# Loading batch 1's k and v after w1's last quarter, and splitting one transpose step of batch 0's q in two

## The chip, the cores and the metric

The kernel runs on one core of a Trainium2 chip. The metric is the device time of one execution in microseconds (us); lower is better. Before the change three runs took 293.19, 293.66 and 294.61 us, a median of 293.66 us. One further execution was recorded by the hardware profiler; all durations below are from it.

## What is computed

The reference is an attention without a score matrix, followed by a two-layer block with a residual. Inputs are q, k, v of shape (8 batches, 8 heads, 576 rows, 64), a gain of 512 and two weight matrices, all in float32.

```
q_s = softmax(q, over the 64 columns)         k_s = softmax(k, over the 576 rows)
kv  = einsum('bhsd,bhse->bhde', k_s, v)       x = einsum('bhsd,bhde->bhse', q_s, kv), heads side by side: (8, 576, 512)
xn  = (x - mean) / sqrt(var + 1e-6) * g_ln    out = x + max(xn @ w_ch1, 0) @ w_ch2     (512 -> 2048 -> 512)
```

## The kernel before the change

**Tiling.** A batch's first 512 rows are four tiles of 128 rows (`j` = 0 to 3). Its last 64 rows, the left-over, are joined with those of the next batch to a fifth tile. Per batch the steps are: softmax of k (maximum over the rows, with a reduction over partitions on GpSimd, subtraction, exponential), `pkv` (the matrix kv of each head on TensorE), softmax of q, transposes of q so that `po` can multiply it by kv, then `x`, `xn`, the transposes `xT`, the first layer `l1`, its `relu`, the second layer `l2`, the final scaling `put` and the `store`. Matmuls run in bfloat16.

**Weights.** `w1l.0` to `w1l.3` load w1 in four quarters of 512 columns, and `w2l.0` to `w2l.3` load w2 in four quarters of 512 rows, each 1 MB of float32 in DRAM, cast to 512 KB of bfloat16 on the way. They are issued by GpSimd (POOL), on a queue of their own (software queue q0). k, v, q and the outputs travel on the queues of SyncE (SP, q1) and ScalarE (ACT, q10). For batch 0 the first layer uses w1 as loaded and the gain is put on the transposed x; afterwards `w1s.0` to `w1s.3` multiply w1's quarters by the gain in place, for all later batches.

**Order.** The order of all work is written out by hand: the string `PROGRAM` is a list of words such as `l2.0.4` or `kl.1.0@SP` (step, batch or chunk, index, and the engine where there is a choice). The words are issued in this order, each to its engine's own instruction stream, and each engine works its stream strictly in order. So a word that has to wait holds back whatever comes after it on the same engine, and nothing on others unless they need its result.

Words that matter here, with the line that the profile shows for them:

- `kl.1.0` (L145) and `vl.1.0` (L151): 1 MB each, batch 1's k and v; `kll.1`, `vll.1` (L124): their left-over rows, 128 KB each; `ql.1.0` (L168): 1 MB of batch 1's q.
- `kmax.1.0` (L184, L187), `kmaxl.1.0` (L194): maximum of batch 1's k on VectorE (DVE); `kar.1.0` (L199): the reduction over partitions on POOL; `ksub.1.1`, `ksub.1.0`, `ksub.1.2` (L217): the subtractions on DVE; `kexp.1.*` (L241): exponentials on ACT; `vc.1.*` (L109): v to bfloat16; `pkv.1.*` (L394).
- `qT.1.2` (L372): transposes of q on TensorE (PE); `qTe.1.2` (L109): their copy out of PSUM on DVE; `zpe.1.2` (L361): eight small matmuls that read this copy and give the softmax sums.
- `l1.0.*` (L552), `l2.0.*` (L592): first and second layer of batch 0. `l2.0.0` to `l2.0.3` read w2's first quarter, `l2.0.4` to `l2.0.7` its second, and so on.
- `w1l` (L511), `w2l` (L530), `w1s` (L519).
- `qT.0.1` (L332), `qTe.0.1` (L109), `zpe.0.1` (L345), `kvb.0.1` (L404, L407): q of batch 0, column chunks 2 and 3, and the normalised kv.
- `warm` (L621): matmuls without a use for their result, which keep PE running.
- `gate.i` (L523): a DMA of 32 bytes on SP that reads a value which another step writes. SP waits for that step before it issues the DMA, and so does all that stands behind it in SP's stream. `gate.2` reads w1's last quarter, so it waits for `w1l.3`.

On PE the words of interest follow each other as `l1.0.14.0, l2.0.0, qT.1.2, l2.0.1, l2.0.2, l2.0.3, zpe.1.2, l2.0.4, ..., l2.0.7, pkv.1.0, pkv.1.1, l2.0.8, ...`; on POOL as `w1l.3, w2l.0, w2l.1, kar.1.0, w2l.2, w2l.3, vc.1.1`.

Of the kernel before, what the change touches and what calls it, by code (L numbers as in the profile page):

```python
# [20 lines left out]
def kernel(  # L21
# [606 lines left out]
    PE, DV, AC, PO, SP = "PE", "DV", "AC", "PO", "SP"  # L628
# [12 lines left out]
        po.0.3 g.1 x.0.0 po.0.1 po.0.2 g.2@AC x.0.3 xn.0.0@AC x.0.1 xn.0.3@AC warm.11.128 xT.0.0  # L641
        xU.0.0 xTe.0.0@DV xTf.0.0@AC warm.4.128 xT.0.3 xU.0.3 xn.0.1@DV l1.0.0.0 xTe.0.3@DV
        xTf.0.3@AC xT.0.1 xU.0.1 x.0.2 l1.0.0.3 xTf.0.1@AC xTe.0.1@DV relu.0.0.0 xn.0.2@DV
        l1.0.0.1 kll.1@AC qmax.1.0 relu.0.0.3 qsub.1.0 xT.0.2 xU.0.2 relu.0.0.1 l1.0.1.1 xTe.0.2@AC xTf.0.2@DV l1.0.1.0 qmax.1.2
        relu.0.1.1 l1.0.1.3 qexp.1.0 qsub.1.2 l1.0.1.2 relu.0.1.3 relu.0.1.0 l1.0.0.2 sq.0.1
# [6 lines left out]
        pkv.1.0 pkv.1.1 kl.2.0@AC l2.0.8 kvb.1.0 l2.0.9 kl.3.0@AC po.1.1 po.1.3 sq.0.0 po.1.2  # L652
        x.1.1 po.1.0 l2.0.10 rstd.0 x.1.0 xn.1.1@AC l2.0.11 x.1.2 xn.1.0@AC x.1.3 l2.0.12
        vl.2.0@AC xn.1.2@AC l2.0.13 qmax.2.0 xT.1.0 put.0.0 l2.0.14 xTe.1.0@AC xn.1.3@DV put.0.1
        l2.0.15 put.0.2 l1.1.0.0 put.0.3 xT.1.2 kmax.2.0 store.0.3@SP l1.1.1.0 xTe.1.2@AC vll.2@SP
        l1.1.2.0 ql.3.0@SP relu.1.0.0 qsub.2.0 l1.1.3.0 relu.1.2.0 relu.1.1.0 l1.1.8.0 kmaxl.2.0
        relu.1.3.0 qmax.2.2 l1.1.9.0 kar.2.0 relu.1.8.0 qexp.2.0 l1.1.10.0 qsub.2.2 relu.1.9.0
        l1.1.11.0 qTd.2.0 ksub.2.2 l1.1.12.0 ksub.2.0 relu.1.11.0 qTd.2.1 relu.1.10.0 l1.1.13.0
        qexp.2.2 ksub.2.1 l1.1.14.0 relu.1.12.0 qTd.2.2 zq.2.0 l1.1.15.0 relu.1.13.0 relu.1.14.0
        l1.1.0.2 qTd.2.3 relu.1.15.0 zq.2.2 l1.1.1.2 relu.1.0.2 kexp.2.1 qll.1.1@SP l1.1.2.2  # L660
        vc.2.1 store.0.0@SP kexp.2.2 l1.1.3.2 store.0.2@SP vc.2.0 kexp.2.0 store.0.1@SP qmax.3.0
        l2.1.0 vc.2.2 qll.1.0@SP relu.1.2.2 l2.1.1 kmax.3.0 relu.1.1.2 kll.3@SP relu.1.3.2 pkv.2.0
        kll.4@SP sq.1.2 pkv.2.1 vl.3.0@SP l2.1.2 kvb.2.0 vll.3@AC l2.1.3 qmax.3.2 po.2.0 po.2.2
        po.2.3 l2.1.4 x.2.0 x.2.3 l2.1.5 xn.2.0@AC x.2.2 xn.2.3@AC xT.2.0 po.2.1 l2.1.6 sq.1.1
        x.2.1 vc.3.2 l2.1.7 qmax.1.4 xn.2.2@AC xT.2.3 kmaxl.3.0 sq.1.3 l2.1.8 xn.2.1@DV sq.1.0
        kar.3.0 xT.2.2 qsub.3.0 l2.1.9 sq.2.0 l2.1.10 xT.2.1 qsub.1.4 rstd.1 qexp.3.0 ksub.3.1
        l2.1.11 kl.4.0@SP sq.2.2 l2.1.12 put.1.0 qTd.3.0 kexp.3.1 l2.1.13 put.1.1 vc.3.1 put.1.2
        qexp.1.4 l2.1.14 vc.3.0 qTd.1.4 l2.1.15 l1.2.0 qTd.3.1 put.1.3 l1.2.1 ksub.3.2 relu.2.0
        ql.4.0@SP ksub.3.0 store.1.1@AC l1.2.2 relu.2.1 l1.2.3 kexp.3.2 qsub.3.2 relu.2.2 l1.2.4
        relu.2.3 kexp.3.0 l1.2.5 kmax.4.0 l1.2.6 relu.2.4 qexp.3.2 l1.2.7 relu.2.5 zq.1.4 qTd.3.3  # L670
        pkv.3.0 relu.2.6 pkv.3.1 store.1.3@AC po.1.4 kvb.3.0 l1.2.8 qTd.3.2 relu.2.7 l1.2.9
        kmaxl.4.0 relu.2.8 ql.5.0@SP zq.3.0 l1.2.10 kar.4.0 gate.3 relu.2.9 store.1.0@SP l1.2.11
        x.1.4 po.3.1 l1.2.12 relu.2.11 zq.3.2 vll.6@SP relu.2.10 vl.4.0@SP l1.2.13 relu.2.12 x.3.1
        sq.2.3 l1.2.14 ksub.4.1 relu.2.13 po.3.2 vll.4@SP po.3.3 xn.1.4@AC l1.2.15 x.3.3
        store.1.2@AC po.3.0 x.3.2 relu.2.14 l2.2.0 gate.0 relu.2.15 ksub.4.0 l2.2.1 sq.3.2
        qmax.4.0 xn.3.1@AC l2.2.2 xn.3.3@AC xT.3.1 l2.2.3 x.3.0 sq.2.1 xn.3.0@DV l2.2.4 qsub.4.0
        rstd.2 xT.3.3 xn.3.2@AC l2.2.5 sq.3.0 ksub.4.2 xT.3.0 l2.2.6 kexp.4.2 l2.2.7 qexp.4.0
        l2.2.8 kexp.4.1 xT.3.2 put.2.1 l2.2.9 qmax.4.2 sq.3.3 kl.5.0@SP vc.4.1 l2.2.10 sq.1.4
        qsub.4.2 kll.5@SP sq.3.1 l2.2.11 vc.4.0 store.2.1@SP l2.2.12 put.2.2 l2.2.13 put.2.0
        store.2.2@SP vc.4.2 l2.2.14 qmax.5.0 qTd.4.0 l2.2.15 l1.3.0 put.2.3 l1.3.1 zq.4.0 relu.3.0  # L680
        qexp.4.2 l1.3.2 qsub.5.0 kexp.4.0 l1.3.3 qTd.4.2 l1.3.4 qmax.5.2 relu.3.1 qTd.4.3 relu.3.2
        pkv.4.0 relu.3.4 zq.4.2 pkv.4.1 relu.3.3 l1.3.5 qTd.4.1 l1.3.6 kvb.4.0 kl.6.0@SP l1.3.7
        kmax.5.0 relu.3.6 kll.6@SP relu.3.5 vl.5.0@SP l1.3.8 relu.3.7 po.4.0 store.2.0@AC l1.3.9
        kmaxl.5.0 relu.3.8 x.4.0 l1.3.10 kar.5.0 relu.3.9 rstd.3 po.4.1 po.4.3 qexp.5.0 l1.3.11
        x.4.1 x.4.3 relu.3.10 l1.3.12 ksub.5.0 relu.3.11 l1.3.13 relu.3.12 sq.4.0 po.4.2 l1.3.14
        x.4.2 xn.4.1@AC l1.3.15 kmax.6.0 relu.3.14 xT.4.1 relu.3.13 l2.3.0 relu.3.15 gate.1 l2.3.1
        xn.4.0@AC kmaxl.6.0 qTd.5.1 qll.3.0@AC l2.3.2 ksub.5.2 xn.4.2@AC xn.4.3@DV qTd.5.0 l2.3.3
        ksub.5.1 sq.4.3 l2.3.4 qsub.5.2 kexp.5.1 xT.4.2 kar.6.0 l2.3.5 qll.3.1@AC put.3.0 vll.5@SP
        l2.3.6 kexp.5.0 store.2.3@SP vc.5.0 ksub.6.2 l2.3.7 xT.4.3 kexp.5.2 kll.7@AC l2.3.8
        put.3.1 qexp.5.2 xT.4.0 l2.3.9 zq.5.0 l2.3.10 qTd.5.3 qmax.3.4 l2.3.11 vc.5.2 vl.6.0@SP  # L690
        l2.3.12 vc.5.1 ql.6.0@SP put.3.2 l2.3.13 qsub.3.4 ksub.6.1 l2.3.14 l2.3.15 kexp.6.1 l1.4.0
        put.3.3 pkv.5.0 relu.4.0 pkv.5.1 sq.4.2 l1.4.1 kvb.5.0 l1.4.2 relu.4.1 zq.5.2 l1.4.3
        vc.6.0 relu.4.2 qexp.3.4 po.5.0 ksub.6.0 po.5.3 vc.6.1 relu.4.3 l1.4.4 qTd.3.4 po.5.1
        zq.3.4 l1.4.5 relu.4.4 qTd.5.2 x.5.0 l1.4.6 vc.6.2 relu.4.5 x.5.3 kexp.6.0 kl.7.0@SP
        l1.4.7 x.5.1 qll.5.1@SP l1.4.8 kexp.6.2 qmax.6.0 ql.7.0@SP relu.4.6 l1.4.9 relu.4.8
        relu.4.7 pkv.6.0 xn.5.1@AC pkv.6.1 po.3.4 relu.4.9 l1.4.10 xT.5.1 x.3.4 l1.4.11 kvb.6.0
        relu.4.10 xT.1.4 l1.4.12 qmax.6.2 relu.4.11 sq.4.1 l1.4.13 store.3.0@SP kmax.7.0 relu.4.12
        qll.5.0@SP po.5.2 l1.4.14 relu.4.13 gate.2 rstd.4 store.3.1@SP l1.4.15 store.3.2@AC x.5.2
        l2.4.0 xn.5.0@DV relu.4.15 kmaxl.7.0 relu.4.14 l2.4.1 qsub.6.2 xn.5.2@AC kar.7.0 l2.4.2
        l2.4.3 ksub.7.1 l2.4.4 store.3.3@AC xn.5.3@AC qsub.6.0 xT.5.0 l2.4.5 kexp.7.1 l2.4.6  # L700
        qmax.7.0 xT.5.3 sq.5.0 l2.4.7 qexp.6.2 xT.5.2 l2.4.8 put.4.1 l2.4.9 put.4.0 qTd.6.2
        qmax.7.2 store.4.0@AC l2.4.10 sq.5.2 l2.4.11 qll.7.0@AC qexp.6.0 l2.4.12 put.4.2 l2.4.13
        qTd.6.0 l2.4.14 qTd.6.1 l2.4.15 l1.5.0 put.4.3 qTd.6.3 l1.5.1 ksub.7.2 relu.5.0 qsub.7.0
        vll.7@SP vl.7.0@AC l1.5.2 store.4.1@SP relu.5.1 l1.5.3 store.4.2@AC qmax.5.4 relu.5.2
        ksub.7.0 l1.5.4 sq.5.3 l1.5.5 relu.5.3 zq.6.0 relu.5.4 l1.5.6 zq.6.2 l1.5.7 relu.5.6
# [477 lines left out]
```

## Time and profile before

| | |
|---|---|
| median of three runs | 293.66 us |
| the profiled execution: its time, its span | 293.68 us, 291.9 us |
| PE busy | 283.0 us (97% of the span) |
| DVE, ACT, POOL busy | 183.3, 172.4, 47.7 us |
| read from and written to DRAM | 36.70 MB, 9.44 MB |
| granted TensorE clock, mean | 1.000 |

The span runs from the first to the last instruction; 1.8 us of the time lie outside it. Times in the views are counted from the span's start. Busy shares are averages over the whole execution: what the change is worth is read from the first 45 us, in which the transfers of batch 0, of batch 1 and of the weights go on together.

### The profile page before, as it was taken

To read this page: it belongs to the slowest core of one execution; us is meant where nothing else is said; L and a number is where in the kernel's file an instruction comes from. 1 tells how busy PE (TensorE), PEld (TensorE's weight loads), DVE (VectorE), ACT (ScalarE), POOL (GpSimd) and SP (SyncE) were. 2 spreads that over 40 slices of the span, in tenths; PEclk is the share of its full clock that TensorE was granted. 3 is DMA by queue.
4 is the path that set the end of the run, shared out by engine and by line. 5 is a ranking of instruction groups with operands and counts; after the bars stand their busy time and mean duration, and the time that the engine had idled before them with its cause. 6 is when DMAs were issued, how large, how long until landed. Compare 5 with 4: busy or idle time off the path is not lost.

```text
span 291.9 us, 4998 instructions
## 1 busy us (share of the span) xinstructions
PE 283.0 (97%) x1952; PEld 145.5 (50%) x1952; DVE 183.3 (63%) x309; ACT 172.4 (59%) x322; POOL 47.7 (16%) x48
## 2 busy tenths in 40 slices
...
GB/s 214 335 247 233 239 222 299 351 224 207 213 225 212 300 197 251 157 274 169 236 166 285 234 121 234 25 98 109 120 19 50 78 124 40 66 42 36 2 30 115
DMA packets 78144, 49.62 MB, mean 170 GB/s; under 512 B 44580, under 2 KB 73640, under 8 KB 78120
## 3 DMA queue, kind: packets, MB, share of 16 engines
...
q10 hardware_dynamic: 12888, 10.36, 12.0%
...
HBM read 36.70 MB, written 9.44 MB: 158 GB/s over the span
## 4 chain that ended last, share of the span: by engine, by line
PE 84%; DMA 12%; POOL 1%; SPq 1%; issue 0%; DVE 0%
PE pc L592 40%; PE ph L538 33%; DMA w_sb<-in_moe_w_ch_dram 9%; PE ph L552 5%; DMA vt<-in_v_dram 3%; PE pot L419 2%; PE pk L394 2%; PE pc L570 1%; POOL v_ab L109 0%; PE pot L428 0%; SPq L174 0%; SPq L145 0%; PE pxt L474 0%; POOL w_sb L530 0%; POOL w_sb L511 0%
## 5 line engine op out<-in xcount | busy, mean ns | idle before, releaser
L592 PE MATMUL pc<-w_sb,hT 128*128 128x512 bf16 x560 | 123.8, 379 | 0.2 <-DMA w_sb<-in_moe_w_ch_dram 0.2
L544 ACT ACTIVATE hT<-ph 128x512 bf16<-128x512 f32 x112 | 63.6, 595 | 60.5 <-PE ph L538 59.9
L538 PE MATMUL ph<-xnT_ab,w_sb 128*128 128x512 bf16 x384 | 87.2, 379 | 0.0
L592 PEld LDWEIGHTS <-hT 128*128 128x128 bf16 x560 | 54.2, 98 | 63.8 <-DMA w_sb<-in_moe_w_ch_dram 0.4
L538 PEld LDWEIGHTS <-w_sb 128*128 128x128 bf16 x448 | 42.8, 98 | 48.7 <-issue 0.2
L602 DVE SCALAR_TENSOR_TENSOR ot<-pc,rstd,x_ab 128x512 f32<-128x512 f32 x32 | 23.2, 745 | 47.3 <-PE pc L592 41.0
L199 POOL PARTITION_ALL_REDUCE km<-kmx x10 | 16.9, 1687 | 85.0 <-DVE kmx L194 76.8
L442 DVE SCALAR_TENSOR_TENSOR x_ab<-pot,rq 128x512 bf16<-128x512 f32 x32 | 21.0, 685 | 13.3 <-PE pot L419 13.1
L552 PE MATMUL ph<-xnT_ab,w_sb 128*128 128x128 bf16 (+2 forms) x256 | 29.2, 272 | 0.0
L466 ACT ACTIVATE xsq<-x_ab,xs_ab 128x512 bf16<-128x512 bf16 x32 | 22.9, 715 | 6.1 <-issue 4.6
L552 PEld LDWEIGHTS <-w_sb 128*128 128x128 bf16 x256 | 19.7, 98 | 8.1
L109 POOL CAST v_ab<-vt 128x1024 bf16<-128x1024 f32 x14 | 18.8, 1360 | 23.5 <-DMA vt<-in_v_dram 16.8
L241 ACT ACTIVATE ek_ab<-kt 128x1024 bf16<-128x1024 f32 x14 | 14.5, 1050 | 11.3 <-DVE kt L217 11.2
L217 DVE TENSOR_TENSOR kt<-kt,km 128x1024 f32<-128x1024 f32 x14 | 18.1, 1307 | 3.7 <-POOL km L199 3.7
L559 ACT ACTIVATE hT<-ph 128x512 bf16<-128x512 f32 x32 | 17.5, 597 | 3.6 <-PE ph L552 3.5
L453 ACT ACTIVATE xn_ab<-x_ab,xs_ab 128x512 bf16<-128x512 bf16 x23 | 15.8, 713 | 3.9 <-DVE x_ab L442 3.4
L300 DVE TENSOR_TENSOR qt<-qt,qm 128x1024 f32<-128x1024 f32 x14 | 17.9, 1277 | 0.2
L295 DVE TENSOR_REDUCE qm<-qt 128x16 f32<-128x1024 f32 x14 | 16.9, 1208 | 0.0
L602 DVE SCALAR_TENSOR_TENSOR ot<-pc,rstd,xl 128x512 f32<-128x512 f32 x3 | 2.2, 747 | 22.0 <-PE pc L592 22.0
L305 ACT ACTIVATE eq_sb<-qt 128x1024 bf16<-128x1024 f32 x14 | 14.7, 1051 | 2.0 <-DMA xnT_ab<-xn_ab 1.7
L353 DVE TENSOR_REDUCE sumq<-eq_sb 128x16 f32<-128x1024 bf16 x12 | 14.4, 1197 | 0.0
L538 PE MATMUL ph<-xnTl,w_sb 128*128 128x512 bf16 x64 | 14.0, 379 | 0.0
...
## 6 DMA issues: line engine op xcount, KB each, us to landing
...
```

The source lines that it names most:

```text
L109: eng.copy(dst, src) if eng is nc.scalar else eng.tensor_copy(dst, src)
L199: nc.gpsimd.partition_all_reduce(self.km[:, hs], self.kmx[:, hs, :D], P, bass_isa.ReduceOp.max)
L217: eng.tensor_tensor(a, a, b, op=ALU.subtract)
L300: eng.tensor_tensor(x, x, t[:, :, :, None].to_broadcast([P, n, H, D]), op=ALU.subtract)
L442: nc.vector.scalar_tensor_tensor(xt.rearrange("p (h d) -> p h d", h=H), in0=self.pot[j], scalar=-1.0, in1=rq[:, :, None].to_broadcast([P, ...
L466: nc.scalar.activation(xsq, xt, AF.Square, bias=xs, scale=-float(DM), accum_out=s)
L538: nc.tensor.matmul(ph, w1_sb[:, ko, m * P:(m + 1) * P], src[:, ko, :], start=(ko == 0), stop=(ko == KO1 - 1),)
L544: nc.scalar.activation(hT[:, m, :], phs[ci, m], AF.Relu)
L552: nc.tensor.matmul(ph[:, i], w1_sb[:, ko, m * P:(m + 1) * P], xnT_ab[:, ci % 2, ko, t * P:(t + n) * P], start=(ko == 0), stop=(ko == KO1 - 1),
L559: nc.scalar.activation(hT[:, c * (4 // n):(c + 1) * (4 // n), t * P:(t + n) * P], phs[ci, c, t], AF.Relu)
L592: nc.tensor.matmul(pcs[ci, ti], hT[:, ko, ti * P:(ti + 1) * P], w2_sb[:, ko, :], start=(ko == 0), stop=(ko == KO2 - 1),)
L602: nc.vector.scalar_tensor_tensor(ots[ci, ti], in0=pcs[ci, ti], scalar=rstd[:, ci, ti:ti + 1], in1=xt, op0=ALU.mult, op1=ALU.subtract,)
```

## The change

Two things are changed, and some words of the order move with them.

1. **Loads of batch 1.** `kl.1.0` and `vll.1` stood ahead of or among the w1 loads, `vl.1.0` after `w2l.1`. Now `vll.1`, `gate.2`, `kl.1.0`, `vl.1.0` stand together behind `w1l.3`. `gate.2` was far back in the list (in the first layer of batch 4); now SP issues batch 1's k and v when w1's last quarter has landed.
2. **q of batch 0, chunks 2 and 3.** One step of eight transposes into one PSUM tile and one copy on ACT become two steps of four transposes (`qT.0.1`, `qU.0.1`), each into a PSUM tile of its own, and two copies: `qTe.0.1` on DVE and `qTf.0.1` on ACT.
3. **Words that move.** `kmax.1.0` goes from ahead of `qTe.1.0` to behind it on DVE; `w1s.0` and `w1s.1` go from behind `zq.1.0` to ahead of `qTe.1.0`; on ACT, `sq.0.2` and `vc.1.2` go ahead of `relu.0.15.0`, `kexp.1.1` ahead of `kexp.1.0`, and `vc.1.0` directly behind `kexp.1.2`.

The core of the diff (the rest of `PROGRAM` is the same words on other lines, without `gate.2`):

```
-        warm.2.128 ksub.0.1 kmaxl.0.2 kar.0.2 qmax.0.0 ksub.0.0 kexp.0.1 kl.1.0@SP w1l.0 ksub.0.2
-        w1l.1 qsub.0.0 vc.0.3@AC w1l.2 vll.1@SP kexp.0.0 ksub.0.4 g.0@AC kexp.0.2 qmax.0.1
-        vc.0.0@PO qexp.0.0 qsub.0.1 kexp.0.4 w1l.3 vc.0.1@AC vc.0.2@AC warm.15.512 pkv.0.0 w2l.0 ksub.0.3
-        pkv.0.1 qexp.0.1 qT.0.0 kvb.0.0 kexp.0.3 warm.6.128 qT.0.1 w2l.1 qTe.0.0@DV
-        vl.1.0@SP pkv.0.2 qTe.0.1@AC zpe.0.0 kvb.0.1 warm.7.128 zpe.0.1 zq.0.0 warm.2.128 po.0.0
+        warm.2.128 ksub.0.1 kmaxl.0.2 kar.0.2 qmax.0.0 ksub.0.0 kexp.0.1 w1l.0 ksub.0.2 w1l.1
+        qsub.0.0 vc.0.3@AC w1l.2 kexp.0.0 ksub.0.4 g.0@AC kexp.0.2 qmax.0.1 vc.0.0@PO qexp.0.0
+        qsub.0.1 kexp.0.4 w1l.3 vll.1@SP gate.2 kl.1.0@SP vl.1.0@SP vc.0.1@AC vc.0.2@AC warm.15.512
+        pkv.0.0 w2l.0 ksub.0.3 pkv.0.1 qexp.0.1 qT.0.0 kvb.0.0 kexp.0.3 warm.6.128 qT.0.1 qU.0.1
+        w2l.1 pkv.0.2 qTe.0.0@DV qTe.0.1@DV qTf.0.1@AC zpe.0.0 kvb.0.1 warm.7.128 zpe.0.1 zq.0.0
...
-        qT.1.0 relu.0.1.2 l1.0.8.0 relu.0.0.2 l1.0.9.0 kmax.1.0 l1.0.11.0 relu.0.9.0 relu.0.8.0
-        l1.0.10.0 relu.0.11.0 qTe.1.0@DV l1.0.13.0 relu.0.10.0 kmaxl.1.0 qexp.1.2 zpe.1.0
-        l1.0.12.0 kar.1.0 l1.0.15.0 relu.0.12.0 relu.0.13.0 l1.0.14.0 w2l.2 ksub.1.1 relu.0.15.0
-        l2.0.0 w2l.3 relu.0.14.0 ksub.1.0 qT.1.2 l2.0.1 ksub.1.2 kexp.1.0 l2.0.2 qTe.1.2@DV
-        kexp.1.1 zq.1.0 w1s.0@DV l2.0.3 kexp.1.2 zpe.1.2 w1s.1@DV l2.0.4 vc.1.2@AC sq.0.2 l2.0.5
-        w1s.2@DV vc.1.0@AC vc.1.1@PO l2.0.6 ql.2.0@AC l2.0.7 zq.1.2 kll.2@AC w1s.3@DV sq.0.3
+        relu.0.1.3 relu.0.1.0 l1.0.0.2 sq.0.1 qT.1.0 relu.0.1.2 l1.0.8.0 relu.0.0.2 l1.0.9.0
+        l1.0.11.0 relu.0.9.0 relu.0.8.0 l1.0.10.0 relu.0.11.0 w1s.0@DV w1s.1@DV qTe.1.0@DV
+        l1.0.13.0 relu.0.10.0 kmax.1.0 kmaxl.1.0 qexp.1.2 zpe.1.0 l1.0.12.0 kar.1.0 l1.0.15.0
+        relu.0.12.0 relu.0.13.0 l1.0.14.0 w2l.2 sq.0.2 vc.1.2@AC ksub.1.1 relu.0.15.0 l2.0.0 w2l.3
+        relu.0.14.0 ksub.1.0 qT.1.2 l2.0.1 ksub.1.2 l2.0.2 qTe.1.2@DV zq.1.0 l2.0.3 kexp.1.1
+        kexp.1.0 kexp.1.2 vc.1.0@AC zpe.1.2 l2.0.4 l2.0.5 w1s.2@DV vc.1.1@PO l2.0.6 ql.2.0@AC
...
-                T["qT", m, i] = task(
-                    lambda e, a, b: s.qT_heads(a, b), ab, (PE,), T["qexp", m, i],
-                )
-                T["qTe", m, i] = task(
-                    s.qTe_heads, ab, (DV, AC), T["qT", m, i],
-                )
+
+                a, b = ab
+                halves = [(a, b)] if i == 0 else [(a, a + 1), (a + 1, b)]
+                for (kt, ke), half in zip((("qT", "qTe"), ("qU", "qTf")), halves):
+                    T[kt, m, i] = task(
+                        lambda e, a, b: s.qT_heads(a, b), half, (PE,), T["qexp", m, i],
+                    )
+                    T[ke, m, i] = task(
+                        s.qTe_heads, half, (DV, AC), T[kt, m, i],
+                    )
                 T["zpe", m, i] = task(
                     lambda e, a, b: s.zpe_heads(a, b), ab, (PE,), T["qTe", m, i],
+                    T.get(("qTf", m, i)),
                     after=T.get(("zpe", m, 0)),
                 )
```

More of the change, by code (lines that the diff above doesn't have):

```diff
@@ L641 @@
[L641 to L645, printed above, removed]
@@ L652 @@
[L652 to L657, printed above, removed]
@@ L658 @@
[L658 to L705, printed above, removed]
@@ L706 @@
-        relu.5.5 l1.5.8 vc.7.2 qsub.7.2 kexp.7.0 po.6.0 l1.5.9 relu.5.7 l1.5.10 x.6.0 relu.5.9
-        relu.5.8 po.6.2 po.6.1 vc.7.0 relu.5.10 l1.5.11 x.6.1 l1.5.12 xn.3.4@DV vc.7.1 relu.5.11
-        x.6.2 l1.5.13 xT.3.4 relu.5.12 kexp.7.2 l1.5.14 sq.6.2 po.6.3 l1.5.15 xn.6.2@AC x.6.3
-        l2.5.0 xn.6.0@DV relu.5.15 xT.6.0 relu.5.14 l2.5.1 relu.5.13 l2.5.2 xT.6.2 sq.5.1 qexp.7.0
-        pkv.7.0 pkv.7.1 l2.5.3 xn.6.1@AC qll.7.1@AC l2.5.4 rstd.5 xn.6.3@AC put.5.0 l2.5.5
-        qexp.7.2 qsub.5.4 xT.6.3 l2.5.6 qexp.5.4 l2.5.7 xT.6.1 l2.5.8 store.4.3@SP l2.5.9 qTd.7.2
@@ L712 @@
-        l2.5.10 qTd.7.3 l2.5.11 l2.5.12 put.5.2 qTd.5.4 l2.5.13 put.5.1 zq.7.0 qTd.7.0 l2.5.14
-        l2.5.15 store.5.1@SP gate.4 l1.6.0 put.5.3 qTd.7.1 l1.6.1 kvb.7.0 relu.6.0 l1.6.2
-        store.5.2@SP qmax.7.4 relu.6.1 sq.6.1 zq.5.4 l1.6.3 relu.6.2 zq.7.2 l1.6.4 store.5.3@AC
-        po.7.0 l1.6.5 relu.6.4 relu.6.3 po.7.3 l1.6.6 relu.6.5 po.7.2 l1.6.7 relu.6.6 x.7.2 l1.6.8
-        x.7.3 relu.6.7 x.7.0 l1.6.9 relu.6.8 qsub.7.4 xn.7.2@AC l1.6.10 sq.6.0 l1.6.11 xn.7.3@AC
-        po.5.4 relu.6.9 xT.7.3 l1.6.12 relu.6.10 relu.6.11 l1.6.13 relu.6.12 l1.6.14 relu.6.13
@@ new lines @@
+        w2l.1 pkv.0.2 qTe.0.0@DV qTe.0.1@DV qTf.0.1@AC zpe.0.0 kvb.0.1 warm.7.128 zpe.0.1 zq.0.0
+        warm.2.128 po.0.0 po.0.3 g.1 x.0.0 po.0.1 po.0.2 g.2@AC x.0.3 xn.0.0@AC x.0.1 xn.0.3@AC
+        warm.11.128 xT.0.0 xU.0.0 xTe.0.0@DV xTf.0.0@AC warm.4.128 xT.0.3 xU.0.3 xn.0.1@DV l1.0.0.0
+        xTe.0.3@DV xTf.0.3@AC xT.0.1 xU.0.1 x.0.2 l1.0.0.3 xTf.0.1@AC xTe.0.1@DV relu.0.0.0
+        xn.0.2@DV l1.0.0.1 kll.1@AC qmax.1.0 relu.0.0.3 qsub.1.0 xT.0.2 xU.0.2 relu.0.0.1 l1.0.1.1
+        xTe.0.2@AC xTf.0.2@DV l1.0.1.0 qmax.1.2 relu.0.1.1 l1.0.1.3 qexp.1.0 qsub.1.2 l1.0.1.2
@@ new lines @@
+        l2.0.7 zq.1.2 kll.2@AC w1s.3@DV sq.0.3 pkv.1.0 pkv.1.1 kl.2.0@AC l2.0.8 kvb.1.0 l2.0.9
+        kl.3.0@AC po.1.1 po.1.3 sq.0.0 po.1.2 x.1.1 po.1.0 l2.0.10 rstd.0 x.1.0 xn.1.1@AC l2.0.11
+        x.1.2 xn.1.0@AC x.1.3 l2.0.12 vl.2.0@AC xn.1.2@AC l2.0.13 qmax.2.0 xT.1.0 put.0.0 l2.0.14
+        xTe.1.0@AC xn.1.3@DV put.0.1 l2.0.15 put.0.2 l1.1.0.0 put.0.3 xT.1.2 kmax.2.0 store.0.3@SP
+        l1.1.1.0 xTe.1.2@AC vll.2@SP l1.1.2.0 ql.3.0@SP relu.1.0.0 qsub.2.0 l1.1.3.0 relu.1.2.0
+        relu.1.1.0 l1.1.8.0 kmaxl.2.0 relu.1.3.0 qmax.2.2 l1.1.9.0 kar.2.0 relu.1.8.0 qexp.2.0
@@ new lines @@
+        l1.1.10.0 qsub.2.2 relu.1.9.0 l1.1.11.0 qTd.2.0 ksub.2.2 l1.1.12.0 ksub.2.0 relu.1.11.0
+        qTd.2.1 relu.1.10.0 l1.1.13.0 qexp.2.2 ksub.2.1 l1.1.14.0 relu.1.12.0 qTd.2.2 zq.2.0
+        l1.1.15.0 relu.1.13.0 relu.1.14.0 l1.1.0.2 qTd.2.3 relu.1.15.0 zq.2.2 l1.1.1.2 relu.1.0.2
+        kexp.2.1 qll.1.1@SP l1.1.2.2 vc.2.1 store.0.0@SP kexp.2.2 l1.1.3.2 store.0.2@SP vc.2.0
+        kexp.2.0 store.0.1@SP qmax.3.0 l2.1.0 vc.2.2 qll.1.0@SP relu.1.2.2 l2.1.1 kmax.3.0
+        relu.1.1.2 kll.3@SP relu.1.3.2 pkv.2.0 kll.4@SP sq.1.2 pkv.2.1 vl.3.0@SP l2.1.2 kvb.2.0
@@ new lines @@
+        vll.3@AC l2.1.3 qmax.3.2 po.2.0 po.2.2 po.2.3 l2.1.4 x.2.0 x.2.3 l2.1.5 xn.2.0@AC x.2.2
+        xn.2.3@AC xT.2.0 po.2.1 l2.1.6 sq.1.1 x.2.1 vc.3.2 l2.1.7 qmax.1.4 xn.2.2@AC xT.2.3
+        kmaxl.3.0 sq.1.3 l2.1.8 xn.2.1@DV sq.1.0 kar.3.0 xT.2.2 qsub.3.0 l2.1.9 sq.2.0 l2.1.10
+        xT.2.1 qsub.1.4 rstd.1 qexp.3.0 ksub.3.1 l2.1.11 kl.4.0@SP sq.2.2 l2.1.12 put.1.0 qTd.3.0
+        kexp.3.1 l2.1.13 put.1.1 vc.3.1 put.1.2 qexp.1.4 l2.1.14 vc.3.0 qTd.1.4 l2.1.15 l1.2.0
+        qTd.3.1 put.1.3 l1.2.1 ksub.3.2 relu.2.0 ql.4.0@SP ksub.3.0 store.1.1@AC l1.2.2 relu.2.1
@@ new lines @@
+        l1.2.3 kexp.3.2 qsub.3.2 relu.2.2 l1.2.4 relu.2.3 kexp.3.0 l1.2.5 kmax.4.0 l1.2.6 relu.2.4
+        qexp.3.2 l1.2.7 relu.2.5 zq.1.4 qTd.3.3 pkv.3.0 relu.2.6 pkv.3.1 store.1.3@AC po.1.4
+        kvb.3.0 l1.2.8 qTd.3.2 relu.2.7 l1.2.9 kmaxl.4.0 relu.2.8 ql.5.0@SP zq.3.0 l1.2.10 kar.4.0
+        gate.3 relu.2.9 store.1.0@SP l1.2.11 x.1.4 po.3.1 l1.2.12 relu.2.11 zq.3.2 vll.6@SP
+        relu.2.10 vl.4.0@SP l1.2.13 relu.2.12 x.3.1 sq.2.3 l1.2.14 ksub.4.1 relu.2.13 po.3.2
+        vll.4@SP po.3.3 xn.1.4@AC l1.2.15 x.3.3 store.1.2@AC po.3.0 x.3.2 relu.2.14 l2.2.0 gate.0
@@ new lines @@
+        relu.2.15 ksub.4.0 l2.2.1 sq.3.2 qmax.4.0 xn.3.1@AC l2.2.2 xn.3.3@AC xT.3.1 l2.2.3 x.3.0
+        sq.2.1 xn.3.0@DV l2.2.4 qsub.4.0 rstd.2 xT.3.3 xn.3.2@AC l2.2.5 sq.3.0 ksub.4.2 xT.3.0
+        l2.2.6 kexp.4.2 l2.2.7 qexp.4.0 l2.2.8 kexp.4.1 xT.3.2 put.2.1 l2.2.9 qmax.4.2 sq.3.3
+        kl.5.0@SP vc.4.1 l2.2.10 sq.1.4 qsub.4.2 kll.5@SP sq.3.1 l2.2.11 vc.4.0 store.2.1@SP
+        l2.2.12 put.2.2 l2.2.13 put.2.0 store.2.2@SP vc.4.2 l2.2.14 qmax.5.0 qTd.4.0 l2.2.15 l1.3.0
+        put.2.3 l1.3.1 zq.4.0 relu.3.0 qexp.4.2 l1.3.2 qsub.5.0 kexp.4.0 l1.3.3 qTd.4.2 l1.3.4
@@ new lines @@
+        qmax.5.2 relu.3.1 qTd.4.3 relu.3.2 pkv.4.0 relu.3.4 zq.4.2 pkv.4.1 relu.3.3 l1.3.5 qTd.4.1
+        l1.3.6 kvb.4.0 kl.6.0@SP l1.3.7 kmax.5.0 relu.3.6 kll.6@SP relu.3.5 vl.5.0@SP l1.3.8
+        relu.3.7 po.4.0 store.2.0@AC l1.3.9 kmaxl.5.0 relu.3.8 x.4.0 l1.3.10 kar.5.0 relu.3.9
+        rstd.3 po.4.1 po.4.3 qexp.5.0 l1.3.11 x.4.1 x.4.3 relu.3.10 l1.3.12 ksub.5.0 relu.3.11
+        l1.3.13 relu.3.12 sq.4.0 po.4.2 l1.3.14 x.4.2 xn.4.1@AC l1.3.15 kmax.6.0 relu.3.14 xT.4.1
+        relu.3.13 l2.3.0 relu.3.15 gate.1 l2.3.1 xn.4.0@AC kmaxl.6.0 qTd.5.1 qll.3.0@AC l2.3.2
```

54 lines of the change are left out of this document (42 added, 12 removed).

## The prediction

> **What bounds the kernel now.** I read the page first, then the waits of PE after 20 us, then the chain of waits, and last the timelines of PE, DVE, POOL and SP's queue up to 45 us.
>
> ```profile
> PE 283.0 (97%) x1952; PEld 145.5 (50%) x1952; DVE 183.3 (63%) x309; ACT 172.4 (59%) x322; POOL 47.7 (16%) x48
> ...
> PE pc L592 <- DMA w_sb<-in_moe_w_ch_dram: 0.2, 1, 0.2
> PE pot L419 <- DVE x_ab L442: 0.2, 1, 0.2
> ```
>
> The second and third line are everything that PE waited for from 20 us to the end. PE is dense from there to its last matmul at 287.8 us, so any wait put into its stream after 20 us is added to the time one for one, and there is almost none to take out.
>
> ```profile
> 15.37 26.03 DMA w_sb<-in_moe_w_ch_dram
> 41.39 0.04 issue
> 41.44 3.61 PE pc L592 x16
> ```
>
> The chain blames a transfer of 26 us: `w2l.1`, issued at 15.37, landed at 41.39, and `l2.0.4` started with it. That looks like a large stall and is not one: PE did other work meanwhile and stood still for some 0.4 us (`zpe.1.2` began at 40.88, `l2.0.4` at 41.44).
>
> ```profile
> 20.00:24.00 4.00, 4.00 (x68) 3.76 (x68) 3.76 (x12) 3.32 (x9) 0.00 (x0) 1.00 1.17 247
> 40.00:44.00 4.00, 3.79 (x25) 1.83 (x24) 4.00 (x15) 3.79 (x8) 1.98 (x1) 1.00 1.24 209
> ```
>
> In these stretches of 4 us the last but one column is the DMA engines' busy share: over 1 (overlapping packets), and so it is in every stretch from 4 to 44 us. Transfers there can be put in another order, not made fewer: what goes first delays the rest. Asked load by load, the landings were: `ql.1.0` 20.8, `kl.1.0` 29.3, `vll.1` and `kll.1` 33.0, `vl.1.0` 41.9; w1's quarters 19.3, 24.6, 28.9, 32.7; w2's 36.9, 41.4, 44.0, 47.1.
>
> ```profile
> 29.36 1.23 DVE L184 TENSOR_TENSOR kmx<-kt 128x1024 f32<-128x1024 f32 x1 [0.62 <-DMA kt<-in_k_dram]
> 30.62 0.69 DVE L187 TENSOR_TENSOR kmx<-kmx 128x512 f32<-128x512 f32 x1
> ...
> 33.09 0.69 DVE L194 TENSOR_TENSOR kmx<-kmx,kl 64x512 f32<-64x512 f32 x1 [1.17 <-DMA kl<-in_k_dram]
> 35.79 2.36 DVE L217 TENSOR_TENSOR kt<-kt,km 128x1024 f32<-128x1024 f32 x2 [2.02 <-POOL km L199]
> 38.18 0.69 DVE L217 TENSOR_TENSOR kl<-kl,km 64x512 f32<-64x512 f32 x1
> 38.90 0.69 DVE L109 COPY qT_sb<-ptr 128x1024 bf16<-128x1024 bf16 x1
> ...
> 36.97 0.55 PEld L592 LDWEIGHTS <-hT 128*128 128x128 bf16 x4 [0.41 <-DMA w_sb<-in_moe_w_ch_dram]
> ...
> 40.88 0.34 PE L361 MATMUL zp<-ones,qT_sb 128*128 128x2 bf16 x8
> ```
>
> This is the part that decides. DVE works batch 1's k (maximum, left-over, then after POOL's reduction the subtractions) and only then copies `qTe.1.2` out of PSUM (38.90 to 39.59), which `zpe.1.2` on PE needs at 40.88. The margin is 1.3 us, with k landed at 29.3.
>
> **The change part by part.**
>
> *When k lands now (L).* Two ways. By totals: all that had landed by 41.9, w2's second quarter among it, still has to pass, and of it only `vl.1.0` is queued behind `kl.1.0`. A 1 MB load alone on the queues takes 3.0 us (landings of the next batches' k: 54.1, 57.1), so L = 41.9 - 3.0 = 38.9; `w2l.2`, issued at 35.63, had part of its 2.6 us (41.4 to 44.0) moved by then, at most some 2.0, so 36.9 from below. By the gate: `w1l.3` landed at 32.7 with `kl.1.0` moved beside it; 3.0 us less gives 29.7. Then SP issues the gate's DMA (median 0.87 us in L523's rows) and `kl.1.0` (0.47), and the load takes 7.3 us (median of SP's k loads) to 8.5 (the time it took beside the weights, 20.8 to 29.3): 38.3 to 39.5. I take **L = 38.3**, bounds 36.9 and 39.5.
>
> *What follows on DVE.* kmax starts 0.06 after landing; its two steps take 1.87 (29.36 to 31.23); from kmaxl to the end of `qTe.1.2` 6.50 (33.09 to 39.59), POOL's reduction in it; 0.1 for the semaphore. That is L + 8.5 = 46.8 for `zpe.1.2`, and 0.2 for its matmuls: `l2.0.4` at 47.0.
>
> *When PE gets there.* `l2.0.0` no longer waits 0.41 for w2's first quarter: 36.56, plus 3.91 (36.97 to 40.88) is 40.5. So PE stands for 6.3 us ahead of `zpe.1.2`, where it had work throughout. Queued behind it on PE is all the rest: `l2.0.4` to `l2.0.7`, whose weights have landed by then, `pkv.1`, and every later batch. `l2.0.4` moves from 41.44 to 47.0: **+5.6 us**, both weight waits already credited.
>
> *TensorE's clock after the stop.*
>
> ```profile
> 2.33 3.40 PE L621 MATMUL idle<-kv_ab,ident 128*128 128x512 bf16 x8 [2.33 <-DVE kv_ab L1126]
> ...
> 9.63 3.41 PE L621 MATMUL idle<-kv_ab,ident 128*128 128x512 bf16 x15
> ```
>
> The same matmul takes 0.425 us after the idle start and 0.227 later (0.216 in the layers): for about the first 3.4 us PE ran at half speed (the clock column shows 1.00 even there, so the durations are the witness). No row shows PE stopped for over 1 us in mid-run: 0.96 us at 13 us cost no speed. So the price is 0 to half of 3.4 us. I take **+1.7 us**, since 6.3 us of standing is nearer to the idle start than to 0.96.
>
> [...]
>
> *w2's third quarter.* On POOL `w2l.2` stands behind `kar.1.0`, which waits for k. Its issue moves from 35.63 to L + 1.93 + 2.54 = 42.8; with its own 8.4 us it lands at 51.2. `l2.0.8` began 4.30 after `l2.0.4`, so it is wanted at 51.3, or 53.0 with the slow clock: nothing added, cover 0.1 to 1.8 us; if gone, each us of lateness costs one.
>
> *v.* `vl.1.0` lands 3.0 after k, at 41.3; its casts (ACT 1.03, POOL 1.98 behind `w2l.3`) end by 48.2, ahead of `pkv.1.0` at about 50.5. Nothing.
>
> *ACT.* `kexp.1.2` ends at about L + 8.7 and the loads of batch 2, behind `vc.1.0`, are issued at 47 where it was 41.91: 5.1 later, while PE is 5.6 to 7.3 later. Their cover is PE's delay. `sq.0.2` and `vc.1.2` (0.9 and 0.6) push `relu.0.15.0` and `relu.0.14.0` to 39.2; their PSUM tiles are wanted from 38.8 and 39.6, in front of PE's stop, which hides it.
>
> *w1s.0, w1s.1 ahead of qTe.1.0.* Eight times 0.27, from the end of the matmuls that read these quarters (29.3): to 31.5, copy to 32.2, `zpe.1.0` at 34.1: covered by 1.9. They fill DVE's wait for k, off the path.
>
> *q of batch 0.* ACT's copy (17.24, 1.01) becomes two of about 0.4 (half of DVE's 0.69, and a fixed part) and 0.6. `zpe.0.1` could start 0.2 to 0.4 sooner, but `warm.7.128` ends at about 18.1 and DVE now has the extra copy ahead of `kvb.0.1`, which ends at 18.7 instead of 18.33; `po.0.0` needs that and began at 18.63. I take 0; bounds -0.4 (the old wait gone) and +0.1.
>
> Sum against the profiled execution, whose time (293.68, span 291.9) stands at the median: 293.7 + 5.6 + 1.7 = **301.0 us**.
>
> **The rivals.**
>
> *The clock stays up.* The 0.96 us stop speaks for it. Then 293.7 + 5.6 = 299.3.
>
> *More comes late.* A weight transfer needs 4.8 us more than its issue to show (w1's first, issued at 9.77, was the slowest per byte, 9.5 us in all); if `w2l.2` takes 2 us more than assumed, or ACT's issues of batch 2 (3.73 us for one of them, with ACT blocked) fall behind PE, a second stop follows: 301.0 + 2.5 = 303.5.
>
> *PE does not wait; not slower.* If w1's last quarter lands so early, with SP's queue empty behind `ql.1.0`, or the gate holds SP so little, that k lands by 32.0, then L + 8.5 is within PE's 40.5 and the gain is real: 0.41 + 0.4 for the two weight waits and up to 0.4 at the q split: 292.5 us. That is the point from which it decides; every us of L beyond it costs one. Against it: w1's four quarters take 2.6 us each even alone, and they share with `ql.1.0` until 20.8, so k behind them at 32.0 would need the queue to run faster than anything in the rows. That the gate does not hold at all gives the same or 293.7.
>
> **How the numbers follow.** Forecast (stop and slow clock) 0.62; clock stays up 0.21; more late 0.08; no wait 0.09. A difference under 0.5% (1.5 us) can hardly be told from none here. The case of no wait lies close to that bound, at 1.2 us, so its chance, rounded to 0.10, is halved between same 0.05 and faster 0.05; slower is the other three, 0.90. The range goes from L = 36.9 with the clock up and the 0.4 of the q split (36.9 + 8.7 - 41.4 = 4.2, less 0.4: 297.5) to L = 39.5 with the slow clock and one us more (6.8 + 1.7 + 1.0: 303.2). The case of no wait is left out.
>
> **What would show it.** In the profile after: kmax of batch 1 (L184) starting near 38.4 instead of 29.36, with DVE idle some 6 us for its DMA; PE's row of eight small matmuls (L361) with an idle of some 6 us ahead of it, put down to DVE's copy (L109); the 16 matmuls L592 behind it taking 5 us instead of 3.6; POOL's issue of w2's second half near 43; no wait of `l2.0.0` or `l2.0.4` for weights. From there on the two timelines should run in step. Wrong would be: kmax starting ahead of 33, PE without a wait of over 2 us, or a second stop at `l2.0.8`.

## The result and the profile after

The change makes the kernel slower: 302.52 us (four runs, 301.75 to 303.0) against 293.55 us, a ratio of 1.0302 (95% interval 1.029 to 1.0314). The forecast was 301.0, range 297.5 to 303.2. The profiled execution took 302.09 us with a span of 300.3, 8.4 us more than before. The page's busy times:

```profile
PE 284.7 (95%) x1922; PEld 146.5 (49%) x1952; DVE 184.8 (62%) x310; ACT 172.0 (57%) x322; POOL 46.2 (15%) x48
```

All that PE waited for from 20 us on (us in total, times, longest):

```profile
PE zp L361 <- DVE qT_sb L109: 6.7, 1, 6.7
PE pc L592 <- issue: 0.2, 1, 0.2
```

Every engine has the work it had, and one wait of 6.7 us has come in: the eight small matmuls of `zpe.1.2` (L361) stand for DVE's copy `qTe.1.2` (L109). The chain of waits names what is behind it:

```profile
13.41 15.63 DMA w_sb<-in_moe_w_ch_dram
29.72 7.75 DMA kt<-in_k_dram
37.49 1.24 DVE kmx L184
40.37 1.79 POOL km L199
42.19 3.49 DVE kt L217 x2
47.53 5.90 PE pc L592 x16
```

w1's last quarter lands at 29.04, SP's gate lets go, k is issued at 29.72 and lands at 37.47 where it was 29.3. Then DVE and POOL work it off, link by link, with nothing beside the chain to hide it. The timeline of the changed kernel (the bracket is the idle time ahead of an instruction and who ended it):

```profile
29.06 0.62 SPq L523 DMA_DIRECT2D gate<-w_sb  x1
...
37.49 1.23 DVE L184 TENSOR_TENSOR kmx<-kt 128x1024 f32<-128x1024 f32 x1 [5.87 <-DMA kt<-in_k_dram]
...
39.48 0.69 DVE L194 TENSOR_TENSOR kmx<-kmx,kl 64x512 f32<-64x512 f32 x1
...
42.03 1.50 POOL L530 DMA_DIRECT2D w_sb<-in_moe_w_ch_dram  x2
42.19 3.48 DVE L217 TENSOR_TENSOR kt<-kt,km 128x1024 f32<-128x1024 f32 x2 [2.02 <-POOL km L199]
...
43.52 1.06 POOL L109 CAST v_ab<-vt 128x1024 bf16<-128x1024 f32 x1
...
47.16 0.37 PE L361 MATMUL zp<-ones,qT_sb 128*128 128x2 bf16 x8 [6.75 <-DVE qT_sb L109]
...
47.40 6.04 PE L592 MATMUL pc<-w_sb,hT 128*128 128x512 bf16 x16
...
53.37 0.83 PE L394 MATMUL pk<-v_ab,ek_ab 128*64 128x65 bf16 x40
```

In the kernel before, `pkv.1.0` stands at:

```profile
44.98 0.83 PE L394 MATMUL pk<-v_ab,ek_ab 128*64 128x65 bf16 x40
```

`l2.0.4` begins at 47.40 instead of 41.44, 5.96 us late. `pkv.1.0` (L394), behind its 16 matmuls, begins at 53.37 instead of 44.98, 8.39 late: the 16 lost another 2.43. From there to the end the two timelines run in step, and 8.4 us is the whole difference of the spans. The stretches around the stop show the granted clock (last but two column) and the busy share of the DMA engines (last but one):

```profile
40.40:45.70 5.30, 0.01 (x1) 0.00 (x0) 3.48 (x3) 1.06 (x2) 4.18 (x4) 0.98 0.45 48
45.80:47.10 1.30, 0.00 (x0) 0.00 (x0) 1.27 (x3) 1.28 (x2) 0.00 (x0) 0.50 1.23 199
47.20:52.50 5.30, 5.30 (x21) 2.05 (x22) 2.34 (x10) 1.96 (x4) 0.00 (x0) 0.52 1.08 252
52.60:56.00 3.40, 3.35 (x54) 1.84 (x54) 1.03 (x3) 1.32 (x4) 0.00 (x0) 1.00 1.15 270
```

The clock fell to half some 5.1 us after PE stopped at 40.41. Stretches of 0.1 us put the fall at 45.5 and the return at 52.3, 6.8 us later. The first row shows something else too: the DMA engines, which in the kernel before were full in every stretch from 4 to 44 us (busy share 1.08 to 1.24), were 0.45 busy while everything waited for k's chain.

### The profile page after: what moved, and what is told of

Its sections match the earlier page's. It is cut to its first block, busy times and chain, and to the rows that moved or that the text cites. A ratio compares the mean times of both kernels' runs of the same rounds, so it can differ in the third digit from the quotient of the medians.

```text
span 300.3 us, 4974 instructions
## 1 busy us (share of the span) xinstructions
PE 284.7 (95%) x1922; PEld 146.5 (49%) x1952; DVE 184.8 (62%) x310; ACT 172.0 (57%) x322; POOL 46.2 (15%) x48
## 4 chain that ended last, share of the span: by engine, by line
PE 82%; DMA 11%; DVE 3%; POOL 1%; SPq 1%; issue 1%; ACT 1%; POOLq 0%
PE pc L592 40%; PE ph L538 32%; DMA w_sb<-in_moe_w_ch_dram 5%; PE ph L552 5%; DMA vt<-in_v_dram 3%; DMA kt<-in_k_dram 3%; PE pot L419 2%; PE pk L394 2%; PE pc L570 1%; DVE kt L217 1%; POOL km L199 1%; DVE kmx L184 0%; PE pot L428 0%; SPq L174 0%; POOL v_ab L109 0%
## 5 line engine op out<-in xcount | busy, mean ns | idle before, releaser
L592 PE MATMUL pc<-w_sb,hT 128*128 128x512 bf16 x544 | 125.1, 384 | 0.9 <-issue 0.2
L538 PEld LDWEIGHTS <-w_sb 128*128 128x128 bf16 x448 | 42.8, 98 | 48.7 <-issue 0.2
L217 DVE TENSOR_TENSOR kt<-kt,km 128x1024 f32<-128x1024 f32 x14 | 19.5, 1403 | 3.7 <-POOL km L199 3.7
L109 POOL CAST v_ab<-vt 128x1024 bf16<-128x1024 f32 x14 | 18.3, 1326 | 17.0 <-DMA vt<-in_v_dram 16.9
L184 DVE TENSOR_TENSOR kmx<-kt 128x1024 f32<-128x1024 f32 (+2 forms) x10 | 10.1, 1006 | 6.5 <-DMA kt<-in_k_dram 6.5
```

The source lines that it names most:

```text
L109: eng.copy(dst, src) if eng is nc.scalar else eng.tensor_copy(dst, src)
L217: eng.tensor_tensor(a, a, b, op=ALU.subtract)
L538: nc.tensor.matmul(ph, w1_sb[:, ko, m * P:(m + 1) * P], src[:, ko, :], start=(ko == 0), stop=(ko == KO1 - 1),)
L592: nc.tensor.matmul(pcs[ci, ti], hT[:, ko, ti * P:(ti + 1) * P], w2_sb[:, ko, :], start=(ko == 0), stop=(ko == KO2 - 1),)
```

## The experiments

The theory: PE lost its time to the late landing of k, through DVE's in-order stream and then the clock. The rivals: the moved words, the split, or w2's second half behind POOL's reduction. Each edit below shows only the words around what changes; the rest of each line, and the code that goes with the split, are left out.

### The gate alone put back

```
-w1l.3 vll.1@SP gate.2 kl.1.0@SP vl.1.0@SP          +w1l.3 vll.1@SP kl.1.0@SP vl.1.0@SP
-relu.4.13 rstd.4                                   +relu.4.13 gate.2 rstd.4
```

> The changed kernel, with gate.2 alone put back to its old place; every other word stays where the change put it, so k and v of batch 1 are issued without waiting for w1's last quarter. Theory (the late landing of k costs the time): k lands near 30 to 32 instead of 37.5, PE stands 0 to 1 us ahead of zpe.1.2, no slow clock: 293.0 to 294.5 us. Rival A (the moved words and the split cost the time): stays above 298 us. Rival B (w2's second half, queued behind the reduction of k, costs it): also falls, but with a stop at l2.0.8.

Measured: 294.49 us, ratio 1.0043 (1.0025 to 1.0061). Taking away one small wait on SP gives back 8.0 of the 9 us, with every moved word in place: rival A falls, and no stop at `l2.0.8` appears, so rival B too. The three longest of PE's waits after 19 us, and DVE's maximum of k:

```profile
PE zp L361 <- DVE qT_sb L109: 0.7, 1, 0.7
PE pc L592 <- DMA w_sb<-in_moe_w_ch_dram: 0.5, 1, 0.5
PE pxt L474 <- ACT xn_ab L453: 0.4, 1, 0.4
```

```profile
32.90 1.22 DVE L184 TENSOR_TENSOR kmx<-kt 128x1024 f32<-128x1024 f32 x1 [1.60 <-DMA kt<-in_k_dram]
```

k, issued at 10.8 behind `vll.1`, landed at 32.9 (expected: 30 to 32), and `zpe.1.2` began at 41.45, 8.55 after it, as the prediction had counted. About 1 us remains. The profiled execution is 0.8 us longer than that of the kernel before: 0.22 are there at `pkv.1.0`, after k landed 3.6 us later; the rest is PE's wait for ACT's `xn`. ACT issued batch 2's two k loads in between, and they took it 7.4 us instead of 5.3.

### The loads' move alone

```
-kexp.0.1 kl.1.0@SP w1l.0        -w1l.2 vll.1@SP kexp.0.0        -vl.1.0@SP pkv.0.2        -relu.4.13 gate.2 rstd.4
+w1l.3 vll.1@SP gate.2 kl.1.0@SP vl.1.0@SP vc.0.1@AC
```

> The kernel before with the move of the four words of the loads alone (vll.1, gate.2, kl.1.0, vl.1.0 behind w1l.3); no split and no other word moved. Theory (late k): DVE's kmax now stands ahead of qTe.1.0, so PE stops earlier, at zpe.1.0 near 34, until about 40.2, and runs slowly after it; l2.0.4 some 8 us late: 301 to 302.5 us. Rival A (the moved words cost the time): 293.5 to 295.

Measured: 302.12 us, ratio 1.0295 (1.0281 to 1.0309). The loads alone do the whole harm. As expected the stop lies earlier, since DVE's maximum of k now stands ahead of `qTe.1.0`:

```profile
40.16 0.37 PE L361 MATMUL zp<-ones,qT_sb 128*128 128x2 bf16 x8 [6.10 <-DVE qT_sb L109]
40.39 5.10 PE L552 MATMUL ph<-xnT_ab,w_sb 128*128 128x512 bf16 x12
```

These are `zpe.1.0` and the last of `l1`, which took 5.10 us; in the kernel before (and in the changed one) they took 2.75. The words that the change moved only decide at which matmul PE stops.

### Gating on w1's second quarter

```
-w1l.3 vll.1@SP gate.2 kl.1.0@SP         +w1l.3 vll.1@SP gate.1 kl.1.0@SP         (gate.2 where gate.1 was)
```

> The changed kernel with gate.1 (waits for w1's second quarter, landed 23.4) in the place of gate.2, and gate.2 in the place of gate.1. Theory (each us of k's landing costs one us of PE): k is issued near 24.5, shares the queues with w1's second half and lands near 34 to 35; PE stands 3 to 3.5 us; 295.5 to 296.5 if the clock stays up in a stop of this length, 298 if it falls. Rival (w1's priority is what costs, whichever quarter gates): as the changed kernel, 302.5.

Measured: 302.34 us, ratio 1.0296 (1.0281 to 1.0312): no gain, against my expectation of 295.5 to 298. SP's queue, DVE and PE:

```profile
24.07 0.58 SPq L145 DMA_DIRECT2D kt<-in_k_dram  x1
...
38.12 1.23 DVE L184 TENSOR_TENSOR kmx<-kt 128x1024 f32<-128x1024 f32 x1 [5.94 <-DMA kt<-in_k_dram]
...
47.79 0.38 PE L361 MATMUL zp<-ones,qT_sb 128*128 128x2 bf16 x8 [6.82 <-DVE qT_sb L109]
```

k was issued 5.6 us sooner and landed at 38.1, no sooner: it took 14.0 us instead of 7.8. I had counted its share of the queues from the moment of issue, but four quarters of w1 and w2, 1 MB each in DRAM, stood issued ahead of it, where in the changed kernel it was two, and all queues together moved some 0.26 MB per us in both (by the totals below). Which of the two quarters gated made no difference (302.34 and 302.52 us), as the rival said, and its reason is right for the start: until 27.5 SP's queue moved next to nothing (5 packets), while POOL's moved 0.68 MB of weights. In the changed kernel SP's queue moved nothing from 29.7 to 32.3 us, then 685 packets beside POOL's 205 up to 35.0 us, and 894 packets alone from there to 37.5. From 24.1 us to k's landing all queues together moved 3.61 MB here and 3.41 MB in the changed kernel. So nearly the same total had to pass until k was through, and that total gave the right landing already in the prediction (36.9 to 38.9). `zpe.1.2` follows k's landing at a steady distance: 9.69 us in the changed kernel (37.47 and 47.16) and here (38.1 and 47.79); 8.55 with the gate put back (32.9 and 41.45), and 8.6 with v's cast on ACT, below (38.3 and 46.90). That experiment shows where the 1.1 us between the two pairs come from.

### Useless matmuls in the stop

```
-vc.1.0@AC zpe.1.2                       +vc.1.0@AC warmb.30.512 zpe.1.2
+    def warmb(n, width):
+        spare = sm_ps.tile([P, DM], FP32, tag="sm", name="spare")
+        for i in range(n):
+            nc.tensor.matmul(
+                spare[:, :width], ident, kv_ab[:, 3, :width // P], start=True, stop=True
+            )
```

> The changed kernel with 30 matmuls of 512 columns, without a use for their result, ahead of zpe.1.2, in a PSUM tile of their own: 30 x 0.216 = 6.5 us of work in the stop of 6.75 us. Theory (after the stop PE runs at half speed until its clock comes back): the 16 matmuls of l2.0.4 to l2.0.7 take 3.5 us again instead of 5.97, all else stays: 302.5 - 2.4 = 300.1 us. Rival (they were slow because of what goes on beside them, DMA or other engines): 302.5, still 5.9 us for the 16.

Measured: 299.84 us, ratio 1.0223 (1.0206 to 1.024), 2.7 us less than the changed kernel.

```profile
39.82 6.64 PE L631 MATMUL spare<-kv_ab,ident 128*128 128x512 bf16 x30
47.09 0.35 PE L361 MATMUL zp<-ones,qT_sb 128*128 128x2 bf16 x8 [0.63 <-DVE qT_sb L109]
47.31 3.61 PE L592 MATMUL pc<-w_sb,hT 128*128 128x512 bf16 x15
```

`zpe.1.2` starts where it did, and the same 16 matmuls (one record is missing from the row) take 3.5 us again, 47.31 to `pkv` at 50.85. The clock was 1.00 throughout, and the DMA share beside them 1.07, where the changed kernel had 1.08: the slow clock after the stop was the second part of the loss, not what runs beside the matmuls.

### v's cast on ACT

```
-vc.1.1@PO                               +vc.1.1@AC
```

> The changed kernel with vc.1.1 (half of batch 1's v to bfloat16) on ACT instead of POOL. In the changed kernel the second subtraction on DVE took about 2.25 us instead of 1.18 while POOL cast v and had just issued w2's second half. Theory (POOL's cast slows DVE): the two subtractions take 2.4 us again instead of 3.48, the stop ends 1.1 us earlier: 301.4 us. Rival (POOL's issue of the w2 loads slows DVE, or DVE slows by itself): still 3.4 us, 302.5.

Measured: 301.17 us, ratio 1.0265 (1.0247 to 1.0283), 1.35 us less than the changed kernel (1.1 by the two ratios to the kernel before).

```profile
43.03 2.36 DVE L217 TENSOR_TENSOR kt<-kt,km 128x1024 f32<-128x1024 f32 x2 [2.02 <-POOL km L199]
...
46.90 0.37 PE L361 MATMUL zp<-ones,qT_sb 128*128 128x2 bf16 x8 [6.28 <-DVE qT_sb L109]
47.13 4.97 PE L592 MATMUL pc<-w_sb,hT 128*128 128x512 bf16 x16
```

The two subtractions take 2.36 us again instead of 3.48, with POOL's issue of w2's second half (42.88 to 44.39) still beside them: POOL's cast, 1.06 us long, had held DVE up by 1.12. By what means, no row shows. In the profiled execution, though, the gain in time is mostly of another kind. k landed 0.8 us later there than in the changed kernel, so `zpe.1.2` began only 0.26 earlier. The slow clock began at 43.1 and was more than half over when PE came back, and the 16 matmuls lost 1.4 us instead of 2.4. So the 301.4 that was expected came out in part by luck; that the earlier slow clock belongs to the edit is not shown.

### The split alone

```
-qT.0.1 w2l.1 qTe.0.0@DV vl.1.0@SP pkv.0.2 qTe.0.1@AC
+qT.0.1 qU.0.1 w2l.1 vl.1.0@SP pkv.0.2 qTe.0.0@DV qTe.0.1@DV qTf.0.1@AC
```

> The kernel before with the split of q's transposes and copies alone. The prediction priced it at 0, with -0.4 as the lower end; the changed kernel's trace shows po.0.0 0.54 us earlier than before, of which 0.24 are earlier q and v loads. Theory now (the split shortens the start): x of batch 0 starts 0.3 to 0.5 us earlier and the time falls by as much, to 293.0 to 293.3. Rival (the earlier start is eaten by the waits for w2's quarters, which are set by the transfers): 293.5, unchanged, with longer waits of l2.0.0 and l2.0.4.

Measured: 293.42 us against 293.38, ratio 1.0004 (0.9995 to 1.0012). Batch 0's first x starts at 18.63 instead of 19.17, and the first layer 0.54 earlier. Of this 0.37 is not the split's: the second transposes of q, which wait for ACT's exponential, began at 16.21 instead of 16.58 in this execution. From them to `po.0.0` it is 1.86 us, against 2.05 in the kernel before; in all profiles at full clock there it is 1.75 to 1.86 with the split and 2.04 or 2.05 without. So the split is worth 0.2 to 0.3 us at this place. Then w2 is not there yet:

```profile
36.88 1.04 PE L592 MATMUL pc<-w_sb,hT 128*128 128x512 bf16 x4 [0.23 <-DMA w_sb<-in_moe_w_ch_dram]
...
41.16 3.61 PE L592 MATMUL pc<-w_sb,hT 128*128 128x512 bf16 x16
```

`l2.0.0` started at 36.97 before. The rival is right: the transfers, not PE, set the pace up to `l2.0.4`, which began at 41.16 when w2's second quarter had landed (41.44 before).

### Only v late

This points to a use of the gate that should not hurt: of batch 1's loads v was the last one to land anyway, and w2 is what PE waits for. So the gate goes ahead of `vl.1.0` alone, k stays in its old place.

```
-w2l.1 vl.1.0@SP pkv.0.2                 +w2l.1 gate.2 vl.1.0@SP pkv.0.2           (and the split, or not)
```

With the split:

> The kernel before with the split, and with gate.2 ahead of vl.1.0 alone: k and the left-overs of batch 1 keep their old places, only v waits for w1's last quarter. Theory (transfers are conserved; what matters is which one is last and how late it is wanted): v was last before too, so it still lands near 42 to 43 although it starts later, w2's first two quarters land 1 to 2 us sooner, PE no longer waits for them and keeps the split's 0.5 us; a wait of pkv.1 for v of up to 0.5 us takes part of it: 292.4 to 293.0 us. Rival (delaying any of batch 1's loads costs time): v lands at 44 or later, pkv.1 waits for over 1.5 us: 294 or more.

Measured: 293.34 against 293.50 us, ratio 0.9998 (0.9976 to 1.0019). v, issued at 33.0 instead of 13.9, landed at 40.3, earlier than the 41.9 before, and PE had no wait for a weight. The time missed the 292.4 to 293.0 that was expected. The runs spread from 292.72 to 295.41 (those of the kernel before, in the same rounds, from 293.22 to 295.99), and in the profiled one the clock fell near the start, so that PE came to `l2.0.0` at 37.95, 1 us later than before:

```profile
16.50:20.00 3.50, 3.20 (x48) 2.94 (x49) 2.57 (x8) 1.35 (x3) 0.00 (x0) 0.53 1.17 246
```

Without the split:

> The same without the split: gate.2 ahead of vl.1.0 is the one change to the kernel before. Theory: the waits of l2.0.0 and l2.0.4 for weights (0.41 and about 0.4 us) go, the later start stays: 292.8 to 293.3 us. Rival (v late costs): 294 or more, with PE waiting at pkv.1.

Measured: 293.23 against 293.50 us, ratio 0.9985 (0.9967 to 1.0003). The weight waits are gone here too, and here the clock is not in the way: v landed at 41.2, and `l2.0.4` began at 41.02 instead of 41.44. In time the gain expected cannot be told from none.

### Only v late, the split, and more useless matmuls at the start

```
-warm.15.512        +warm.18.512         -warm.6.128        +warm.12.128
```

> v late and the split, and more matmuls without a use ahead of the two waits of PE in batch 0 (18 instead of 15 of 512 columns ahead of pkv.0.0, 12 instead of 6 of 128 ahead of qT.0.1): 0.65 and 0.33 us more work in waits of 0.9 and 0.5 us. In the profile of v late with the split the clock fell to half between 16.5 and 20 us, with no stop of over 0.9 us near it; its runs spread from 292.7 to 295.4. Theory (the spread is the clock falling in these waits): the runs draw together at 292.6 to 293.0, below the kernel before. Rival (the spread comes from the transfers): the spread stays, and where v of batch 0 is early the added work costs up to 0.6: 293.5.

Measured: 293.11 against 293.57 us, ratio 0.9983 (0.9975 to 0.9992); the runs lie between 292.86 and 293.30, a little above the 292.6 to 293.0 that was expected. This version is a little faster than both kernels, by 0.5 us against the kernel before. The control, the same matmuls in the kernel before:

> The kernel before with the same added matmuls alone. Both theories: 293.3 to 293.6, unchanged, since w2's quarters set the pace after the start; it tells whether the added work by itself gains or costs anything.

Measured: 293.47 against 293.57 us, ratio 0.9998 (0.9989 to 1.0007). So the added matmuls do nothing by themselves. That the runs of the v-late version drew together fits the clock's fall seen in one of its profiles, but the cause is not shown: there is one profile of each, and these rounds, on another chip, were quieter for the kernel before too (293.31 to 293.81, against 293.22 to 295.99).

## Why the prediction was right, point by point

Both terms of the sum were the right ones, and both came out larger. The profiled execution took 302.09 us, 1.1 more than the 301.0: 0.36 of it from the stop, 0.73 from the clock.

- **When k lands.** Forecast 38.3 (36.9 to 39.5), measured 37.5. Of the way by the gate: w1 landed at 29.0 (29.7), from there to k's issue it was 0.7 (1.34), the load took 7.75 (7.3 to 8.5). The 1.34 had two faults: the gate's 0.87 was a median of other places in the kernel (0.62 here), and k's own issue of 0.47 is part of the load's time already, which the profile counts from the start of the issue.
- **What follows on DVE.** Forecast 8.5 from landing to `zpe.1.2`, measured 9.7. Mis-sized by the two subtractions: POOL's cast of v, which the prediction placed behind w2's issue without asking what it does to DVE, fell on them. Moved to ACT, the same way takes 8.6.
- **PE's arrival.** Forecast 40.5, measured 40.4 (47.16 less the idle 6.75). The stop was forecast at 6.3 us and was 6.75; `l2.0.4` +5.6 and was +5.96, two errors of about 1 us having cancelled in part.
- **The clock.** The direction was right and the size too small: 1.7 forecast, 2.43 measured, above the most (half of 3.4) that the prediction allowed. It took the 3.4 us of slow matmuls at the kernel's start for the length of the slow state; around the stop that lasted 6.8 us. That the clock fell to half in the stop, 5.1 us after it began, and was back 5.2 us after PE had begun again is shown by the stretches of 0.1 us; with the useless matmuls in the stop it stayed at 1.00. In the run with v's cast on ACT the same two times were 2.5 and 3.0 us: neither was the same in both runs; the 6.8 us between the fall and the return was.
- **w2's third quarter.** Issued at 42.03 (42.8) and landed 6.1 us later (8.4 assumed), at 48.1, wanted at 54.1: no wait, as forecast, with more cover than the 0.1 to 1.8.
- **q of batch 0.** Forecast 0, with -0.4 as the lower end; the split's own share, 0.2 to 0.3 us earlier at `po.0.0`, lies inside these bounds. Mis-sized was the extra copy on DVE, which was to end `kvb.0.1` 0.37 later (18.7): counted from DVE's first copy, `kvb.0.1` ended after 1.72 us instead of 1.56, so it cost 0.16. The time did not move all the same, for a reason that the prediction had half in hand: it had seen the two waits for w2, but took only the removal of these waits for a gain and did not see that they swallow an earlier start.
- **The rivals.** A clock that stays up (299.3) is what the 30 useless matmuls give: 299.84. No second stop came. A kernel where PE does not wait needed k by 32.0; with the gate put back and k landing at 32.9 the wait was 0.7.
